# Fifteen small loads in front of the last value tile of a decode attention kernel

## The chip, the cores and the metric

The kernel runs on one core of one Trainium2 chip. The metric is the device time of one execution in microseconds (us). The kernel before took 657.95 us (median of 2 runs, 657.61 to 658.3). Single executions of the same kernel differ by some tenths of a microsecond, and now and then by 2 or 3.

TensorE is called PE below, VectorE DVE, ScalarE ACT, GpSimd POOL and SyncE SP, as in the profile. "The trace" is the record of one execution, and it also lists every packet that the DMA engines moved and the moment at which each engine reported a load as landed. It does so by a small write, the load's completion, which raises a semaphore: a counter for which other engines can wait.

## The reference

One decode step: attention with 16 query heads on 8 key/value heads over caches of 8192 positions, beside a small gated MLP.

```python
# x (4, 1, 448); k_cache, v_cache (4, 8, 8192, 256); all bf16
q = (xn @ wq) as 16 heads of 256
scores = einsum("bhqd,bhkd->bhqk", q, k) / 16
o = einsum("bhqk,bhkd->bhqd", softmax(scores), v)
s = o @ wo
g = silu(mlp_block(xn))            # small weights
return x + s * g
```

There are 32 key tiles and 32 value tiles of 4 MB (4 batches x 8 heads), 268 MB in all. Every byte is used once.

## The kernel before

SyncE issues all the large loads, in one queue. Each key tile goes into one of two buffers, each value tile too. The last value tile is cut into four pieces, and the last four heads' output weights are loaded behind it in three loads.

```python
def load_v(h):                              # ... marks a cut
    b, g = where(h)
    src = A_v_cache[b, g].rearrange("(p c) d -> p c d", p=P)
    if h < NH - 1:
        sp.wait_ge(S["v_v"], h + 1)
        sp.dma_start(vflat[h % 2], ...).then_inc(S["dv%d" % (h % 2)], 16)
    else:                                   # the last value tile, in four pieces
        sp.wait_ge(S["v_k"], h)
        for i in range(NPIECE):
            lo, hi = PIECES[i], PIECES[i + 1]
            sp.dma_start(kn[:, 1 - h % 2, lo:hi, :]..., ...).then_inc(S["dvl%d" % i], 16)

...
for h in range(2, NH):
    load_k(h)
    load_v(h - 2)
load_v(NH - 2)
load_v(NH - 1)
for i, hs in enumerate(LATE):               # output weights of the last heads
    load_wo(hs[0], hs[-1] + 1, "dwl%d" % i)
sp.wait_ge(S["v_out"], 1)                   # the result is ready
store(sp, 0)
take(sp, "dout", 16 * NDG)                  # the store has landed
...
def take(eng, name, n=1):                   # wait for n, and take n away
    eng.wait_ge(S[name], n).then_inc(S[name], -n)
...
# PE, at the very end
take(pe, "dwl0", 16)
f_o(LATE[0])
take(pe, "v_ot")
f_o(range(HQ - REP, HQ))
for i in range(1, len(LATE)):
    take(pe, "dwl%d" % i, 16)
    ins = f_o(LATE[i], i == len(LATE) - 1)
```

So the end of the kernel is a chain: last landings, a few matmuls, two DVE operations, the store, the waits of SyncE after the store, and the barrier that closes the program.

## Time and profile before

| | before |
|---|---|
| time | 657.95 us |
| span of the trace | 656.9 us |
| load queue, share of 16 engines' time | 99.2% |
| PE, DVE, ACT busy | 85%, 42%, 39% |
| landing of the last weight load, first to last engine | 650.29 to 652.59 us |

From the page of the kernel before: busy time of PE; the mean busy share of the DMA engines in 40 slices of the span, in tenths; the rate in the same slices; the count of packets; and the load queue (packets, MB, share of the time of 16 engines).

```profile
PE 556.3 (85%) x9937; PEld 476.3 (73%) x9937; DVE 276.5 (42%) x589; ACT 256.0 (39%) x364; POOL 13.4 (2%) x77
DMA  8999999999999999999999999999999999999996
GB/s 360 440 413 425 434 427 437 425 439 427 437 427 435 429 435 431 431 435 427 437 429 433 429 433 429 433 429 433 429 435 431 433 431 435 429 433 433 429 425 256
DMA packets 12353, 279.13 MB, mean 425 GB/s; under 512 B 1204, under 2 KB 3256, under 8 KB 3768
q1 hardware_dynamic: 12328, 278.99, 99.2%
```

The DMA engines hardly rest, so it is they that should set the time.

The timeline of SyncE (start, duration, issue, how many):

```profile
599.26 20.76 SPq L212 DMA_DIRECT2D vb<-in_A_v_cache_dram  x2
620.07 1.85 SPq L219 DMA_DIRECT2D kn<-in_A_v_cache_dram  x4
621.96 11.71 SPq L229 DMA_DIRECT2D wo_sb<-in_A_wo_dram  x3
654.88 0.35 SPq L186 DMA_DIRECT2D out_dram<-out_b  x1
```

The second of the two value tiles in the first line is issued at 619.7 us, directly ahead of the four pieces; the new loads go between. The data of these pieces moves only from about 637 us on, so SyncE runs some 17 us ahead of the engines. One of the three weight issues stands for 10.7 us, as if the queue took no more.

The chain that ended last (start, duration, what):

```profile
651.61 2.42 PE pst L687 x24
654.06 0.39 DVE res L526
654.47 0.38 DVE out_b L528
```

### The profile page before, as it was taken

How to read it: one execution, taken by the hardware profiler on the slowest of the kernel's cores; microseconds unless marked ns; L12 is line 12 of the kernel's file. 1: busy time of each engine (PE TensorE's matmuls, PEld its weight loads, DVE VectorE, ACT ScalarE, POOL GpSimd, SP SyncE). 2: the span in 40 equal slices, each digit the busy share in tenths (PEclk: the TensorE clock that was granted, in tenths of full speed). 3: DMA queues.
4: the chain of work that ended last, by engine and by line, in shares of the span. 5: the costliest groups of instructions: out<-in, count | busy, mean ns of one | idle time of the engine just before them, and what ended most of it. 6: DMA issues, size and time to landing. Idle time of an engine off the chain costs nothing. (4 is left out here: it accounts for less than half of the span.)

```text
span 656.9 us, 22864 instructions
## 1 busy us (share of the span) xinstructions
PE 556.3 (85%) x9937; PEld 476.3 (73%) x9937; DVE 276.5 (42%) x589; ACT 256.0 (39%) x364; POOL 13.4 (2%) x77
## 2 busy tenths in 40 slices
PE   1899997988888988888897888898888889888897
PEld 0487886876766887667787766798767678766775
DVE  7353554443443444434443443444334443433442
ACT  4144544442433443323444333444333344433340
POOL 2000000000000000000000000000000000000000
PEclk9698999887899878889987888988878987887998
DMA  8999999999999999999999999999999999999996
GB/s 360 440 413 425 434 427 437 425 439 427 437 427 435 429 435 431 431 435 427 437 429 433 429 433 429 433 429 433 429 435 431 433 431 435 429 433 433 429 425 256
DMA packets 12353, 279.13 MB, mean 425 GB/s; under 512 B 1204, under 2 KB 3256, under 8 KB 3768
## 3 DMA queue, kind: packets, MB, share of 16 engines
q1 hardware_dynamic: 12328, 278.99, 99.2%
q8 instruction: 7, 0.11, 0.1%
q14 instruction: 2, 0.02, 0.0%
q10 hardware_dynamic: 16, 0.01, 0.0%
HBM read 278.99 MB, written 0.00 MB: 425 GB/s over the span
## 5 line engine op out<-in xcount | busy, mean ns | idle before, releaser
L588 PE MATMUL pst<-ident_b,kn 128*128 128x128 bf16 x4096 | 347.3, 239 | 78.6 <-PEq L245 76.3
L295 ACT ACTIVATE kT<-pst 128x1024 bf16<-128x1024 bf16 x224 | 229.3, 1024 | 360.6 <-ACTq L245 359.5
L588 PEld LDWEIGHTS pst<-ident_b,kn 128*128 128x128 bf16 x4096 | 275.4, 108 | 84.3 <-issue 83.8
L293 DVE COPY kT<-pst 128x1024 bf16<-128x1024 bf16 x288 | 197.5, 691 | 263.7 <-DVEq L245 263.7
L600 PE MATMUL psc<-qc,kT 128*128 128x2 bf16 x4096 | 178.7, 165 | 0.0
L600 PEld LDWEIGHTS psc<-qc,kT 128*128 128x128 bf16 x4096 | 157.7, 98 | 28.5 <-issue 28.3
L639 PE MATMUL psv<-vb,pT 128*4 128x512 bf16 x1056 | 86.4, 378 | 0.3 <-issue 0.3
L618 PE MATMUL psm<-sel,po 128*128 128x2 f32 x272 | 36.8, 257 | 0.5 <-PEq L245 0.5
L618 PEld LDWEIGHTS psm<-sel,po 128*128 128x128 f32 x272 | 34.8, 197 | 0.9 <-issue 0.9
L639 PEld LDWEIGHTS psv<-vb,pT 128*4 128x4 bf16 x1056 | 22.3, 82 | 15.3 <-issue 0.8
L452 DVE TENSOR_REDUCE rmax<-psc 128x2 f32<-128x128 f32 x32 | 9.3, 292 | 48.8 <-DVEq L245 48.8
L470 DVE COPY po<-psv 128x512 f32<-128x512 f32 x34 | 23.5, 692 | 3.0 <-DVEq L245 2.3
L457 DVE TENSOR_REDUCE gmax<-psm 2x1 f32<-2x128 f32 x32 | 8.9, 279 | 34.7 <-DVEq L245 34.7
L317 ACT ACTIVATE pT<-psc,negb 128x64 bf16<-128x64 f32 x66 | 20.6, 331 | 5.4 <-ACTq L245 5.4
L612 PEld LDWEIGHTS psm<-diag,ones_f 2*128 2x128 f32 x66 | 14.1, 263 | 6.4 <-issue 5.4
L280 POOL COPY qc<-qT 128x4 bf16<-128x4 bf16 x32 | 5.9, 186 | 585.8 <-DVEq L469 568.6
L612 PE MATMUL psm<-diag,ones_f 2*128 2x2 f32 x66 | 16.8, 321 | 1.1 <-PEq L245 0.9
L317 ACT ACTIVATION_READ_ACCUMULATOR pT<-psc,negb 128x1 f32 x66 | 13.6, 206 | 0.0
L608 PEld LDWEIGHTS psm<-ident_f,rmax 128*2 128x2 f32 x32 | 2.6, 80 | 14.0 <-issue 14.0
L536 PE MATMUL pst<-ident_b,xn_b 4*128 4x4 bf16 x14 | 0.6, 161 | 13.6 <-DVE xn_b L365 8.9
L630 PE MATMUL psm<-rowsum,ones_f 128*128 128x2 f32 x64 | 11.6, 251 | 0.0
L536 PEld LDWEIGHTS pst<-ident_b,xn_b 4*128 4x128 bf16 x14 | 0.5, 100 | 13.6 <-issue 8.9
(101 smaller groups left out, 122.4 us busy)
## 6 DMA issues: line engine op xcount, KB each, us to landing
kn<-in_A_k_cache_dram SPq DMA_DIRECT2D x32, 4096.0 KB, 25.7
vb<-in_A_v_cache_dram SPq DMA_DIRECT2D x31, 4096.0 KB, 31.3
vb<-in_A_wq_dram SPq DMA_DIRECT2D x1, 3584.0 KB, 11.7
vb<-in_B_w_dram SPq DMA_DIRECT2D x2, 1568.0 KB, 16.6
wo_sb<-in_A_wo_dram SPq DMA_DIRECT2D x1, 2688.0 KB, 44.3
kn<-in_A_v_cache_dram SPq DMA_DIRECT2D x1, 2048.0 KB, 25.2
kn<-in_A_v_cache_dram SPq DMA_DIRECT2D x1, 1024.0 KB, 27.3
kn<-in_A_v_cache_dram SPq DMA_DIRECT2D x2, 512.0 KB, 28.5
```

Source lines behind the costliest of these rows:

```text
L293: engine.tensor_copy(dst, src).then_inc(S["v_ev"], 1)
L295: engine.activation(dst, src, ACT.Copy).then_inc(S["a_ev"], 1)
L317: ins = act.activation(pv_p[:, :, hh], sc[:, :, hh], ACT.Exp, bias=negb[:, s, hh:hh + 1], scale=SCALE, accum_out=rowsum[:, s, hh:hh + 1])
L452: v.tensor_reduce(rmax[:, :], psc[h % 2][:, 0:NCH * REP].rearrange("p (k h) -> p h k", h=REP), AX.X, ALU.max).then_inc(S["v_rmax"], 1)
L457: v.tensor_reduce(gmax[:, :], psm[0:REP, 0:P], AX.X, ALU.max).then_inc(S["v_s"], 1)
L470: v.tensor_copy(po[:, slot], psv[:, 0:CP * DH]).then_inc(S["v_po"], 1)
L588: ins = pe.transpose(dst[:, t * P:(t + 1) * P], kn[:, h % 2, GC * j + kl, half * P:(half + 1) * P], ident_b[:, :])
L600: ins = pe.matmul(psc[h % 2][:, kk * REP:(kk + 1) * REP], kT[:, j % RING, t * P:(t + 1) * P], qc[:, h % 2, half, :], start=(half == 0), st ...
L612: pe.matmul(psm[:, P:P + REP], ones_f[0:REP, :], diag[:, :], start=True, stop=True).then_inc(S["p_m2"], 1)
L618: ins = pe.matmul(dst(dh)[:, 0:width], po[:, slot, i * DH + dh:(i + 1) * DH:NHALF], sel[:, i, 0:width], start=(i == 0), stop=(i == CP - 1))
L630: pe.matmul(psm[:, P + REP:P + 2 * REP], ones_f[:, :], rowsum[:, h % 2, :], start=True, stop=True)
L639: ins = pe.matmul(psv[o:o + CP * REP, 0:CP * DH], pT[:, h % 2, kk * REP:(kk + CP) * REP], src[:, kk:kk + CP, :].rearrange("p c d -> p (c d)"),
```

## The change

Fifteen loads of 1, 2, ... 15 rows of 44 bytes are put between the last two value tiles, into buffers that are no longer used. Nothing reads them. All fifteen take their rows from the start of the same key tile. Load n is meant to occupy the first n of the 16 DMA engines, so the engines get 15, 14, ... 1, 0 extra rows. SyncE waits for them after the store.

```diff
-            + ["dvl%d" % i for i in range(NPIECE)] + ["dwl%d" % i for i in range(len(LATE))]
+            + ["dvl%d" % i for i in range(NPIECE)] + ["de%d" % i for i in range(15)] + ["dwl%d" % i for i in range(len(LATE))]
@@
             load_v(NH - 2)
+            for i in range(15):
+                room = (gel_u, gel_a, gel_b)[i // 5][:, :].bitcast(BF16)
+                sp.dma_start(room[0:i + 1, i % 5 * 22:(i % 5 + 1) * 22],
+                             A_k_cache[0, 0, 0:i + 1, 0:22]).then_inc(S["de%d" % i], 16)
             load_v(NH - 1)
@@
             store(sp, 0)
             take(sp, "dout", 16 * NDG)
+            for i in range(15):
+                take(sp, "de%d" % i, 16)
```

## The prediction

> **What bounds the kernel now.** The DMA engines. On the page the DMA row is 9 in nearly every slice, the mean is 425 GB/s, and the load queue took 99.2% of 16 engines' time; PE is busy 85%, VectorE 42%. Among the trace's DMA packets a 32 KB row takes 1.22 us, a completion write 9 ns, and the next packet of that engine starts at once. Packets of 448, 1792, 4096 and 8192 bytes took 26, 75, 160 and 314 ns: about 9 ns plus 0.037 ns per byte. The engines are not in step: the 16 landings of each 4 MB tile spread over 2.45 us, those of the last weight load over 2.3 (650.3 to 652.6 us). Then come matmuls (2.4 us in the chain of waits, partly before that landing), two VectorE operations of 0.38, the store (landed at 656.3), and SyncE's closing waits.
>
> **What the change adds.** Fifteen loads in SyncE's queue after the value tile issued at 619.7 us; nothing is removed. By the Trainium skill (DMA: Bandwidth & Descriptors, "Why a DMA increments its semaphore by 16 and not by 1") a load uses the largest k up to 16 that divides its outer size, on the lowest-numbered engines: load n uses n engines, one row each. So the first engine gets 15 rows and 15 completions, the fifteenth one of each, the sixteenth none. No run shows this yet.
>
> Estimates from the numbers above:
> - Engines: a 44-byte row 11 ns, with its completion 20, so 0.3 us on the first engine, less on the others. The skill (same page, "Specifications") has transfers under 512 B as read-modify-write; even trebled, that is under 1 us. The trace shows no pause after completions. What reaches the end depends on which engine is last in the spread, which I can't tell: 0 to 0.6 us.
> - SyncE: an issue takes 0.33 to 0.43 us, start to start up to 0.47, so 5 to 7 us. The pieces of the last value tile, issued now at 620.1 to 621.5, move to 626 to 629; the engines reach them after 637. Hidden.
> - Queue room: the last weight load's issue took 10.7 us (623.0 to 633.7), as if the queue held 60 to 70 descriptors per engine. The first engine's 30 more will make the last pieces and weight loads wait for room until about 640 to 645; needed from 645 to 649. Hidden, but the nearest thing to a real loss.
> - The end: fifteen more SyncE waits after the store has landed, met long before but run one after another. Its step from the last wait to the next instruction is 80 ns; 15 x 40 to 80 ns = 0.6 to 1.2 us, all on the critical path.
>
> **Predicted:** 659.2 us: 0.9 for the waits, about 0.3 for the engines; 8 in 10 between 657.4 and 662.5. Faster by over 2%: 0.5%; within 2%: 96.5%; slower by over 2%: 3%.
>
> **What would show it.** Right: 120 more 44-byte packets of 10 to 40 ns; landings of the last tile under 1 us later, spread about 2.5; DMA row still 9; 15 more SyncE waits after the store, about 1 us; the blocked issue ends after 638 us. Wrong: a DMA gap between 637 and 650 us (queue ran dry), or packets after the small rows starting over 1 us late.
>
> **What would make it wrong.** Small rows handled one at a time with a full memory round trip each: 15 of 1 to 2 us on the first engine would be 15 to 30 us, over 2%.

## More of the kernel before

Busy time by stage near the end (stretch, length, busy us and count by engine, granted PE clock, DMA share, GB/s):

```profile
core 0: us, PE busy (x) PEld busy (x) DVE busy (x) ACT busy (x) POOL busy (x), PEclk, DMA share, GB/s
635.00:640.00 5.00, 4.06 (x59) 1.87 (x57) 1.56 (x5) 0.70 (x4) 0.00 (x0) 1.00 0.97 416
650.00:657.00 7.00, 3.52 (x47) 2.95 (x46) 0.94 (x3) 0.00 (x0) 0.00 (x0) 0.62 0.14 50
```

Keep the 0.62 in mind: the trace's record of the clock has it at full speed until 651.67 us and at half from there on, so in this execution PE was throttled during the last matmuls.

## The result, and the profile after

The changed kernel took 659.58 us (659.38 to 659.78, 2 runs). The ratio is 1.0028, with a 95% interval of 1.0010 to 1.0047. (A ratio is the mean time of one kernel's runs over that of the other's of the same rounds, so not quite the ratio of the medians quoted.) A second measurement with 6 runs gave 660.11 us against 657.90, ratio 1.0032 (1.0018 to 1.0047). The interval excludes zero, and the loss is about 2 us.

The same lines of the page after:

```profile
PE 557.4 (85%) x9937; PEld 477.5 (73%) x9937; DVE 274.5 (42%) x589; ACT 256.1 (39%) x364; POOL 13.6 (2%) x77
DMA  8999999999999999999999999999999999999996
GB/s 362 441 415 422 435 426 436 428 432 432 430 434 430 434 426 438 424 438 426 434 432 428 432 430 434 430 434 426 436 430 430 434 426 436 430 432 430 434 404 250
DMA packets 12594, 279.14 MB, mean 424 GB/s; under 512 B 1444, under 2 KB 3496, under 8 KB 4008
q1 hardware_dynamic: 12568, 279.00, 99.1%
```

The load queue has 240 packets more (12568 less 12328): 120 rows and 120 completions. The DMA digits are unchanged, but the last rate but one fell from 425 to 404 GB/s. A busy share can't show a packet that takes longer; the rate does.

The timeline of SyncE after:

```profile
599.15 21.03 SPq L212 DMA_DIRECT2D vb<-in_A_v_cache_dram  x2
620.23 1.56 SPq L239 DMA_DIRECT2D gel_u<-in_A_k_cache_dram  x5
621.84 1.65 SPq L239 DMA_DIRECT2D gel_a<-in_A_k_cache_dram  x5
623.92 1.92 SPq L239 DMA_DIRECT2D gel_b<-in_A_k_cache_dram  x5
625.88 1.81 SPq L219 DMA_DIRECT2D kn<-in_A_v_cache_dram  x4
627.74 10.03 SPq L229 DMA_DIRECT2D wo_sb<-in_A_wo_dram  x3
654.99 0.29 SPq L186 DMA_DIRECT2D out_dram<-out_b  x1
```

The fifteen issues cost SyncE 5.7 us, and the last pieces are issued at 625.9 in place of 620.1 us. The engines reach them at about 637.6, so this is hidden.

The chain that ended last, and the stages near the end:

```profile
652.66 1.47 PE pst L693 x24
654.16 0.40 DVE res L532
654.58 0.38 DVE out_b L534
```

```profile
core 0: us, PE busy (x) PEld busy (x) DVE busy (x) ACT busy (x) POOL busy (x), PEclk, DMA share, GB/s
635.00:640.00 5.00, 4.06 (x59) 1.88 (x58) 1.57 (x5) 0.70 (x4) 0.00 (x0) 1.00 0.96 358
650.00:657.00 7.00, 3.38 (x64) 2.90 (x64) 1.51 (x4) 0.00 (x0) 0.00 (x0) 0.89 0.24 91
```

Between 635 and 640 us, where the small rows are moved, the rate fell from 416 to 358 GB/s at the same DMA share.

Do not compare the two chains alone. The last matmuls start 1.05 us later after, yet the matmul group ends only 0.10 us later (654.13 against 654.03), as if the later landing had cost nothing. The reason is the clock: over the group alone the granted clock was 0.52 before (651.60 to 654.00 us) and 1.00 after (652.70 to 654.10), and the same 24 matmuls took 2.42 and 1.47 us. That this was chance is shown by the control runs below; in the traces of all other runs the group had the full clock.

The landings of the small loads in the trace after, in us, one number for each increment of the load's semaphore (listed from the trace, not a view of the profile):

```
load of  1 row : 620.682 (at issue) | 638.081
load of  2 rows: 621.010 (at issue) | 638.264 638.586
load of  3 rows: 621.306 (at issue) | 638.446 638.763 639.403
load of  4 rows: 621.619 (at issue) | 638.626 638.944 639.284 639.578
load of 15 rows: 626.009 (at issue) | 639.468 639.687 639.838 ... 641.552 642.203   (15 landings)
```

Two things are read here. Load n lands on exactly n engines, and one increment comes at once, at issue. This is what the Trainium skill says (DMA: Bandwidth & Descriptors, "Why a DMA increments its semaphore by 16 and not by 1"): a load takes k engines, k the largest number up to 16 that divides its outer sizes, and the issuing sequencer writes the missing 16 - k itself. And on the first engine the landings follow each other at 638.081, 638.264, 638.446, 638.626: one every 0.18 us.

### The profile page after: what moved, and what is told of

Same layout as the page of the kernel before. It is cut to its first block, busy times and chain, and to the rows that moved or that the text cites. A ratio compares the mean times of both kernels' runs of the same rounds, so it can differ in the third digit from the quotient of the medians.

```text
span 657.7 us, 22894 instructions
## 1 busy us (share of the span) xinstructions
PE 557.4 (85%) x9937; PEld 477.5 (73%) x9937; DVE 274.5 (42%) x589; ACT 256.1 (39%) x364; POOL 13.6 (2%) x77
## 3 DMA queue, kind: packets, MB, share of 16 engines
q1 hardware_dynamic: 12568, 279.00, 99.1%
## 5 line engine op out<-in xcount | busy, mean ns | idle before, releaser
L636 PEld LDWEIGHTS psm<-rowsum,ones_f 128*128 128x128 f32 x64 | 9.5, 188 | 0.0
```

Source lines behind the costliest of these rows:

```text
L636: pe.matmul(psm[:, P + REP:P + 2 * REP], ones_f[:, :], rowsum[:, h % 2, :], start=True, stop=True)
```

## The experiments

**Two theories.** Theory 1: about half of the loss is the fifteen waits, run one after another at the very end, and half is the DMA engines, each delayed by its small loads, the latest engine deciding. Rivals: the whole loss is in the loads (the waits vanish in the closing barrier); or the loads disturb the queue or all engines together. Within the engines' part there is a second question: what costs 0.18 us, the short row or the load's completion?

A time of 660 us repeated to some tenths can hardly separate parts of 1 us, so the argument uses two intervals of each trace, which repeat to about 0.02 us in the controls (the runs were made on three chips; each of them has a run with a tail of 12.19 or 12.20):

- *tail*: from the last landing of the last value tile but one, behind which the small rows stand in every engine's queue, to the last landing of the last weight load (the earlier engines move their small rows before the latest has landed that tile, which matters for two runs below);
- *close*: from the store's landing to the end of the span.

| run | time, us (n) | before in the same rounds | ratio (95%) | tail, us | close, us |
|---|---|---|---|---|---|
| first trace before | 657.95 (2) | | | 12.18 | 0.56 |
| before_again | 657.95 (6) | 657.90 | 1.0001 (0.9987 to 1.0015) | 12.19 | 0.56 |
| first trace after | 659.58 (2) | 657.95 | 1.0028 (1.0010 to 1.0047) | 13.26 | 1.33 |
| after_again | 660.11 (6) | 657.90 | 1.0032 (1.0018 to 1.0047) | 13.25 | 1.33 |
| waits_early | 658.87 (6) | 657.90 | 1.0019 (1.0003 to 1.0035) | 13.10 | 0.30 |
| waits_only | 659.34 (6) | 657.90 | 1.0019 (1.0003 to 1.0035) | 12.20 | 1.30 |
| all16 | 659.91 (5) | 658.08 | 1.0027 (1.0013 to 1.0040) | 14.52 | 0.31 |
| one_load | 658.25 (5) | 658.08 | 1.0001 (0.9987 to 1.0015) | 12.29 | 0.34 |
| all16_512 | 660.39 (5) | 658.08 | 1.0033 (1.0019 to 1.0047) | 14.44 | 0.30 |
| row_ones | 657.78 (5) | 658.08 | 0.9995 (0.9981 to 1.0008) | 12.20 | 0.30 |
| all16_n4 | 657.73 (6) | 657.87 | 0.9992 (0.9978 to 1.0006) | 12.30 | 0.31 |
| all16_n30 | 663.07 (6) | 657.87 | 1.0075 (1.0061 to 1.0090) | 17.52 | 0.30 |
| spread15 | 658.11 (6) | 657.87 | 1.0001 (0.9986 to 1.0016) | 12.22 | 0.31 |
| two_more | 657.86 (6) | 657.87 | 0.9995 (0.9980 to 1.0009) | 12.19 | 0.34 |

All experiments gave correct results.

### Controls: before_again, after_again

Edit: none.

> The kernel before, unchanged, as a control. All theories: ratio 1.000 within 0.2%; last weight load landed at about 652.6 us in the trace with a spread of about 2.3 us over the engines; the last matmul ends within 1.5 to 2.5 us after its fifth-last wait, depending on the clock granted in the last 7 us (0.62 in the first trace). If that clock is different now, the 2.4 us of the last matmul group in the first trace were chance and not a property of the kernel.

> The changed kernel, unchanged, as a control with an interval of its own. All theories: 1.2 to 2.0 us over the kernel before, 1.0 us of it the fifteen closing waits (67 ns each), the rest the later landing of the last weight load (about 653.6 us).

The group of the last matmuls in the chain of before_again, then of after_again:

```profile
651.57 1.48 PE pst L687 x24
```

```profile
652.83 1.50 PE pst L693 x24
```

With the full clock in both (it fell to half only at 655.7 and 657.3 us, after the group) the group takes the same time, so the 2.42 us of the first trace were chance, and the later landing reaches the end in full. The accounting of these two traces: span 655.86 and 657.93 us, difference 2.07. Of that, 0.22 was there already when the last value tile but one had landed (chance: at the key tile that landed at about 524 us the difference was already 0.23); the tail gave 1.06; from the last weight landing to the last matmul's end 0.50 us in both; the close gave 0.77. The sum is 2.05. The difference of the times, 2.2 us, lies a little above the 1.2 to 2.0 expected for after_again.

### Waits: waits_early, waits_only

Edit of waits_early, and of waits_only:

```diff
+            for i in range(15):
+                take(sp, "de%d" % i, 16)
             sp.wait_ge(S["v_out"], 1)
             store(sp, 0)
             take(sp, "dout", 16 * NDG)
-            for i in range(15):
-                take(sp, "de%d" % i, 16)
```

```diff
             load_v(NH - 2)
-            (the fifteen small loads)
             load_v(NH - 1)
@@
+            for i in range(15):
+                sp.sem_inc(S["de%d" % i], 16)
             sp.wait_ge(S["v_out"], 1)
             store(sp, 0)
             take(sp, "dout", 16 * NDG)
             (the fifteen waits stay)
```

> The changed kernel with its fifteen waits moved from after the store to before the wait for the result, where SyncE idles. Theory 1 (the waits cost 1.0 us of the 1.6, the engines the rest): 1.0 us faster than the changed kernel, 0.3 to 1.0 us slower than the kernel before. Rival (the waits are hidden in the closing barrier, the loss is all in the loads): no faster than the changed kernel.

> No small loads, but the fifteen waits after the store, on semaphores that SyncE raises itself beforehand. Theory 1: 0.7 to 1.0 us slower than the kernel before, with the last landing unchanged at about 652.6 us. Rival (all in the loads): the same as the kernel before within 0.2 us.

Moved to where SyncE idles, the waits cost nothing: close 0.30 us in place of 1.33, while the tail stays long, at 13.10 (0.15 less than in after_again, which was not explained). Alone, they cost what they cost in the changed kernel: close 1.30, tail 12.20 as before. So theory 1 holds and the rival falls. The starts of SyncE's instructions in after_again, in ns (listed from the trace), show the size: one wait every 67 ns, though every one had been met 14 us earlier.

```
656612 wait for the store     656688 wait de0    656774 wait de1    656840 wait de2
656907 wait de3  ...          657640 wait de14   657713 drain       657866 last barrier wait
```

One point of the expectation for waits_only missed: the last landing came at 653.88, not 652.6. But in that execution the last value tile but one was already 1.3 us late (641.68 against 640.34), so it is chance from earlier in the run; this is why the interval is used and not the moment. The time missed as well, 1.4 us above the kernel before (by the ratio 1.2) in place of 0.7 to 1.0; its interval, 0.03% to 0.35%, holds the expected loss.

### What the 0.18 us belong to: all16, one_load, all16_512

Edits against waits_early; `room` is a new tile, so rows start on 256 or 512 bytes:

```diff
 all16
-                sp.dma_start(room[0:i + 1, i % 5 * 22:(i % 5 + 1) * 22],
-                             A_k_cache[0, 0, 0:i + 1, 0:22]).then_inc(S["de%d" % i], 16)
+                sp.dma_start(room[0:16, i, 0:22],
+                             A_k_cache[0, 0, 0:16, 0:22]).then_inc(S["de%d" % i], 16)
 one_load (no loop, one wait)
+            sp.dma_start(room[:, :, 0:22],
+                         A_k_cache[0, 0, 0:240, 0:22].rearrange("(p c) d -> p c d", p=16)
+                         ).then_inc(S["de0"], 16)
 all16_512
+                sp.dma_start(room[:, i, :] if i < 14 else q_b[0:16, 0:256],
+                             A_k_cache[0, 0, 0:16, 0:256]).then_inc(S["de%d" % i], 16)
```

> Fifteen loads of 16 rows of 44 bytes, so every one of the 16 engines gets 15 rows and 15 completions; waits hidden as in waits_early. Theory A (each small load costs its engine about 0.18 us, of which the first four or so are absorbed, so 2.06 us for fifteen): every engine's landings of the last pieces 1.9 to 2.4 us later than before, spread back to about 2.4 us, last landing at about 654.7 us, time 1 to 2.1 us over the kernel before. Theory B (a packet of 44 bytes costs only its 11 ns and its completion 9, and the later landing in the changed kernel has another cause): landings at most 0.3 us later.

> One load of 240 rows of 44 bytes, 15 rows for each of the 16 engines as in all16, but one completion for each engine instead of 15. If the 0.18 us belong to the completion[...]: landings at most 0.4 us later than before. If they belong to the short row (under 512 bytes): landings about 2 us later, as in all16.

> As all16, but with rows of 512 bytes. If the cost is that of rows under 512 bytes: landings only about 15 x (28 + 9 ns) = 0.5 us later than before. If it is the completion's: as all16, 2 us or somewhat more.

In all three, each of the 16 engines moves 15 extra rows. With 15 completions the tail is 2.33 us longer than in before_again (14.52 less 12.19). With one completion for 240 rows of the same size it is 0.10 us longer, with rows of 512 bytes 2.25.

In the last two runs the tail misses a part. There the last value tile but one itself landed 9.92 and 10.13 us after the value tile before it, against 9.72 to 9.77 in all other traces. Counted from that earlier tile, last landing to last landing, the extra over before_again is 2.34 us for all16, 0.29 for one_load and 2.65 for all16_512. The 0.31 more for the longer rows is about what they take themselves: they are listed with 27 ns in place of 11, which is 0.24 us for fifteen. So the cost goes with the separate loads, not with the short rows. One rival was not tested: in all16 and all16_512 every load reads the same 16 rows of the cache again, while one_load reads 240 different ones, so a cost of reading the same rows again so soon would look the same.

Two details of the expectation for all16 missed slightly: the last piece's landings spread over 2.13 us, not 2.4, and its first landing was 2.55 us later than in before_again, not 1.9 to 2.4.

The stretch from 636 to 646 us of before_again, all16 and one_load, in this order (columns as above; the last is GB/s):

```profile
636.00:646.00 10.00, 8.53 (x103) 5.20 (x97) 2.75 (x9) 0.70 (x4) 0.00 (x0) 1.00 0.96 408
```

```profile
636.00:646.00 10.00, 8.52 (x100) 5.27 (x98) 2.66 (x9) 0.70 (x4) 0.00 (x0) 1.00 0.96 318
```

```profile
636.00:646.00 10.00, 8.52 (x107) 5.34 (x107) 2.61 (x8) 0.70 (x4) 0.00 (x0) 1.00 0.96 391
```

PE and the others do the same work in these 10 us, the DMA share is the same, only the rate differs. Where does the loss hide in the packets? In all16 the 240 small rows are listed with 11 ns each and their completions with 9, and the next large packet starts at once. But that packet, 16 KB, is then listed with up to 2189 ns, against 611 in the usual case. What the 16 KB packets took beyond 611 ns is 1.91 us for each engine (mean; 0.03 in before_again), and with the listed 0.30 us of the small rows and completions that is most of the 2.34. The engine accepts the small rows quickly and pays afterwards, so the prediction's argument ("The trace shows no pause after completions") looked in the wrong place.

### Engines are separate: row_ones

Edit against waits_early: every load has one row.

```diff
+                sp.dma_start(room[0:1, i, 0:22],
+                             A_k_cache[0, 0, 0:1, 0:22]).then_inc(S["de%d" % i], 16)
```

> Fifteen loads of one row, all on the first engine, which is the earliest of the 16 by 2.4 us. Theory (engines are separate queues, and a delay counts only when it passes the latest engine): the first engine's landings about 2 us later, the last landing of all unchanged within 0.15 us, the spread no larger, and the time that of the kernel before within 0.3 us. Rival (small loads disturb all engines or the issue): last landing later by 0.5 us or more.

All fifteen loads fall on the first engine. One 16 KB packet of the tail took 1928 ns and another 1127, while the median of all was 615; so that one engine was held back by 1.8 us, about as in the changed kernel (longest packet 1931). The tail is 12.20 us, that is unchanged, and the time too. The first engine is ahead of the latest by more than 2 us (in the trace after, the first small row landed on it at 638.081, and on the latest of the fifteen engines, the seventh, at 640.568), and its delay disappears in that lead. The rival, a disturbance of all engines or of the issue, falls. One caution: in the traces of row_ones, all16_n4 and all16_n30 the last matmul ended 0.91, 1.03 and 0.66 us after the last landing, not 0.50, because PE was still at earlier work. PE is thus only some tenths behind the DMA engines at the end, another reason to judge by the tail and not by the time.

### How the cost grows: all16_n4, all16_n30, spread15

Edits against all16: 4 loads, or 30 loads with two on each semaphore (and their rows 224 bytes apart in the buffer). In spread15 the fifteen loads stand in the loop, three after each value tile of its last five turns:

```diff
             for h in range(2, NH):
                 load_k(h)
                 load_v(h - 2)
+                for i in range(max(0, 3 * (h - NH + 5)), max(0, 3 * (h - NH + 6))):
+                    sp.dma_start(room[0:16, i, 0:22],
+                                 A_k_cache[0, 0, 0:16, 0:22]).then_inc(S["de%d" % i], 16)
             load_v(NH - 2)
-            (the fifteen loads)
```

> As all16 with 4 loads in place of 15. From the last landing of the last value tile but one to the last landing of the last weight load the kernel before takes 12.19 us and all16 14.52. If every completion costs its engine the same 0.155 us (2.33 / 15): 12.8 us. If the first four or so are absorbed, as the engines with 1 to 4 rows of the changed kernel suggest: 12.2 to 12.4 us, and the time of the kernel before within 0.3 us.

> As all16 with 30 loads (two on each semaphore). If the cost beyond the first four is a constant 0.18 to 0.21 us for each load, the same interval is 17.0 to 17.8 us; if the cost is a fixed one of having many small loads at all, about 14.5 us. Over 18 us would mean that the queue ran dry, since 60 more descriptors stand in it on each engine.

> The same fifteen 16-row loads as all16, but three after each of the value tiles in the last five turns of the loop, so that 4 MB tiles lie between the groups. If completions are absorbed up to about four in a row and the engine catches up while it moves large rows: the kernel before within 0.3 us, and no packet after the small rows over 0.2 us longer than usual. If each completion has a fixed cost wherever it stands: about 2 us over the kernel before, as all16.

The tail is longer than that of before_again by 0.11 us for 4 loads, 2.33 for 15 and 5.33 for 30. From 4 to 15 that is 0.20 us for each load, from 15 to 30 again 0.20; the line meets zero at about 3.4 loads. So the first three or so in a row are nearly absorbed, and each further one costs its engine 0.20 us. With three between 4 MB tiles, fifteen loads cost nothing that the clock can show: spread15 has the time of the kernel before, and from 540 us on its longest packets of 32 KB are 1241 ns, against 1228 before (but for one of 1640 beside a fetch of instructions, as all16 has one too). The trace shows a little. From the landing of a key tile at about 524 us, before any small row, to the last weight landing, spread15 took 129.12 us, and the four traces without small loads 128.75 to 128.79. The 0.33 to 0.37 us more are about the 15 x 20 ns at which the rows and completions are listed; all16 took 131.12.

### The closing step: two_more

Edit against the kernel before:

```diff
+            sp.sem_inc(S["de0"], 16)
+            take(sp, "de0", 16)
             sp.wait_ge(S["v_out"], 1)
             store(sp, 0)
```

> The kernel before with two more SyncE instructions (raise a semaphore and take it back) before the wait for the result; no loads. In both traces of the kernel before the last SyncE instruction started 445 ns after the one before it, in all eight others, which have more SyncE instructions, 153 ns. If the length of the SyncE program sets this: 153 ns here too, the span 0.29 us shorter from the store's landing to the end, and a time 0.1 to 0.4 us under the kernel before (hardly to be told apart by the clock). If the small loads or their waits set it: 445 ns.

SyncE's last step was 153 ns, as expected, and the close 0.34 us in place of 0.56 (0.22 shorter; 0.29 was expected). So a longer SyncE program, not the loads, makes the close shorter by 0.2 to 0.3 us. The time, 657.86 against 657.87 us, does not show it: no version here beats the kernel before by the clock. Why the two instructions help was not settled; a fetch of instructions, in a DMA queue of its own, comes only 0.6 us after the end of the span in both traces of the kernel before, and before the end of the span in the changed kernels, and of two_more, which would fit, but no run moved that fetch alone.

## Why the prediction was right or wrong

The number was right: 659.2 us predicted, 659.58 measured (660.11 in the larger sample), inside 657.4 to 662.5, and within 2% as forecast. Its steps:

- **"The DMA engines bound the kernel": right.** A change of 1.06 us in the last landing moved the end by as much once the clock was equal.
- **"Load n uses n engines": right**, seen in the landings.
- **"SyncE ... 5 to 7 us. Hidden": right.** The issues took 5.7 us and moved the pieces to 625.9; the tail of row_ones, with the same issues, was unchanged.
- **"Queue room ... until about 640 to 645": right that it is hidden, wrong in size.** The issues of the weights stood for 4.67 and 4.84 us and were through at 637.8, ahead of the predicted "after 638". Counted in the trace, about 76 packets per engine had not begun when the blocked issue ended before, and 85 after, not 60 to 70.
- **"The end: 0.6 to 1.2 us": right.** Fifteen waits at 67 ns are 1.0 us; the net of the close was 0.77, because the close is 0.2 to 0.3 us shorter for another reason.
- **"A 44-byte row 11 ns, with its completion 20, so 0.3 us on the first engine ... 0 to 0.6 us": the step that failed.** The packets were indeed 11 and 9 ns, and still each load beyond about three cost its engine 0.20 us. For the latest engine, the seventh, which had nine small loads, this gives 0.20 x (9 - 3.4) = 1.1 us; the tail grew by 1.06. The term of 0.3 us was about 1.1. As a sum of listed packets the step holds only where few small loads stand together: spread15 cost about 0.35 us.
- **"Even trebled" for short rows: the wrong suspect.** Rows of 44 bytes cost no more than rows of 512 (2.34 and 2.65 us for fifteen loads).
- **"Landings of the last tile under 1 us later, spread about 2.5": wrong**, as follows from the same step: 1.07 us later (651.44 against 650.37), spread 3.29 us.

The sum came out well partly by luck: the engines' term was too small by 0.8 us, and nothing had been taken off for the shorter close. It stayed small because the first engines, which got most of the loads, were on the whole not the last to finish, and because only the latest engine counts. all16, with fifteen for every engine, lost 2.33 us in its tail.

Left open: whether the 0.20 us belong to the completion, to starting a new load, or to reading the same rows again. one_load removes all three together. Why about three are absorbed is open as well.

## What to carry to other kernels

Count loads, not bytes: where the DMA engines were the limit here, every small load beyond three or so in a row cost each engine that it used 0.20 us, and one load with many rows, or small loads spread between large ones, cost about 0.3 us for fifteen rows on every engine (that reading the same rows again has a part in the 0.20 us is not excluded). A packet's listed time can be innocent and the packet after it pays, so compare rates and landings, engine by engine, and remember that only a delay of the latest engine reaches the end. Waits that had long been met still cost 67 ns each at the end of the program; put them where the engine idles.

## What the Trainium skill lacked or had wrong

- DMA: Bandwidth & Descriptors, "Anatomy of one DMA — SWDGE (gpsimd) path", says that "The trn2 sem-write bubble is tiny (~1 cycle)". That section is about loads issued by GpSimd; these were issued by SyncE, so no run here contradicts it. Carried over to them it would mislead: the completions are listed with 9 ns, and still loads of one row for each engine, in a row, took 0.20 us of each engine's time for every load beyond about three. The page has no figure for this.
- The same page, "Specifications", gives 512 bytes as the least transfer for full rate, with read-modify-write below. In these runs the short rows cost nothing extra that could be seen: fifteen loads with rows of 44 bytes cost 2.34 us, with 512 bytes 2.65, and 240 rows of 44 bytes under one load 0.29.
- The same page, "Rules for kernel authors", says to coalesce small transfers; it doesn't say that what counts is the number of loads in a row, nor that three between large tiles are nearly free (spread15: about 0.35 us for fifteen loads, ratio 1.0001).
- No page that was read gives the cost of a wait that is already met: 67 ns each on SyncE.
- No page that was read says how much can stand in SyncE's queue before an issue is held up: an issue stood for 10.7 us in the trace before, and two for 4.67 and 4.84 us in the trace after.
